# Regrouping k and q of the next batch earlier, and loading v in a step of its own, in a fused attention and mixer kernel

## The chip, the cores and the metric

The kernel runs on one core of one Trainium2 chip. The metric is device time in microseconds (us), from the start to the end of one execution; lower is better. The kernel is written with a manual schedule: each engine executes its instructions in the order in which the program issues them, and engines wait for each other through semaphores that the framework places where tiles are written and read. The engines are TensorE (PE in the profile), VectorE (DVE), ScalarE (ACT), GpSimd (POOL) and SyncE (SP). SP and POOL issue the DMAs.

## The reference

For 8 batches, 12 heads, 448 tokens and a head width of 64, a sigmoid attention without normalisation is followed by an MLP mixer over tokens and channels (d_model 768, token width 256, channel width 1536):

```
scores = (q @ k.T) / sqrt(64) - log(448)
x      = sigmoid(scores) @ v                    # heads side by side: 448 x 768 a batch
u      = x + (relu(x.T @ w_tok1) @ w_tok2).T
out    = u + relu(u @ w_ch1) @ w_ch2
```

Inputs and output are float32; the kernel loads and multiplies in float16 and accumulates in float32.

## The kernel before, in words

A batch is cut into three **units** (u = 0, 1, 2) of four heads. A **cycle** c = 3b + u works at unit u of batch b. The opening (cycles 0 to 5) and three cycles of transition (6 to 8, lines 1082 to 1138) lead to the main loop (cycles 9 to 23, batches 3 to 7, lines 1147 to 1206), whose order of work on PE is the table STEPS (lines 1141 to 1145), one row a unit. Its letters:

- **k**: one block of scores (qk, line 187): four matmuls of tr_k against tr_q into a PSUM tile, and a sigmoid on ACT (line 199) into one buffer of the ring att, 10 deep.
- **a4, a7**: attention times v (av, line 209) for the unit of the cycle before. DVE then casts the sum into xT (line 228), and after a7 SP issues a DMA transpose of xT into xn (xtrans_dma, line 241). In unit 2, a7 also has token_sums, four differences of u on DVE (line 446).
- **t, T**: the first token matmul (tok_tail, line 276, and tok1, line 295), reading the xn that was transposed one cycle earlier. At the end of each cycle ytrans (line 311) does the second token matmul, and DVE adds it to xT in the tile ut (line 325).
- **7** (unit 2 only): utrans (line 330), a DMA transpose of the whole ut into un (the rows of u that are added to the output), and sevens (line 1071), the 15 steps of the first channel matmul for the batch before, by seven products of sums (line 503). sums are combinations of c1, hsums of c2, made once from the weights (weight_sums, output_sums; lines 407 and 619); the list early holds these 24 pieces of DVE work, of which c2's are the last 12.
- **q6, r, L, 4, 5, 6**: second channel matmul of the batch before that (lines 373, 692, 712, 753). DVE adds un to the result (lines 576, 732, 778) and SP stores the output rows (line 589).
- **c**: takes up to two pieces from the list copies.

The list **copies** prepares k and q of the next batch. At the end of unit 0 it is filled by through_dma(b + 1, 0) (line 152) with eight pieces: three regroupings of k by DVE (relayout, line 134: raw_k to rel_k, one a unit), one DMA transpose of rel_k into tr_k (line 147, issued by SP), and then the same four for q. Before the change, unit 1 takes two at its first c (k0, k1) and two at the c that ends it (k2 and k's transpose); unit 2 takes two at its c (q0, q1), and sevens takes the last two after its steps 1 and 3 (q2, and q's transpose). So on SP's queue q's transpose stands behind un's.

Loads are issued by POOL (load, line 118), two DMAs a tensor and batch, with the cast from float32 to float16 on the way. gated_loads(b) (line 988), at the end of unit 2, first has POOL copy two elements of tr_q of batch b + 1 (line 990); that copy can only run when q's transpose has landed, and it holds back everything behind it on POOL's queue: v of batch b + 1, then k and q of batch b + 2. raw_k and raw_q have one buffer each, raw_v two.

Of the kernel before, what the change touches and what calls it, by code (L numbers as in the profile page):

```python
# [9 lines left out]
FP16 = mybir.dt.float16  # L10
# [11 lines left out]
NJ = 7  # L22
NP = 64
NU = 3
# [6 lines left out]
def kernel(  # L31
# [11 lines left out]
    nc = tc.nc  # L43

    B, H, S, E = q.shape
# [15 lines left out]
    pa = ctx.enter_context(tc.tile_pool(name="pa", bufs=2))  # L61
# [7 lines left out]
    c2 = pc.tile([128, NCB, D], FP16, name="c2")  # L69
    gate = pc.tile([128, 2], FP16, name="gate")  # L70
# [31 lines left out]
    raw, rel, tr = {}, {}, {}  # L102
    att, xn, h1, un = {}, {}, {}, {}
# [14 lines left out]
    def load(b, t, src, u0, u1):  # L118

        for g in range(2):  # L120
            dst = raw_tile(b, t)[64 * g : 64 * g + 64, u0:u1, :, :, :]
            heads = src[b, 6 * g + 2 * u0 : 6 * g + 2 * u1]
            nc.gpsimd.dma_start(
                out=dst.rearrange("p u hi j e -> p (u hi) (j e)"),
                in_=heads.rearrange("h (p j) e -> p h (j e)", j=NJ),
            )
# [58 lines left out]


    def qk(b, u, j):
        att[b, u, j] = pa.tile([128, 2, S], FP16, tag="att", bufs=10, name=f"att_{b}_{u}_{j}")
        ps = pp.tile([128, 2, 512], FP32, tag="qk", bufs=2, name=f"qk_{b}_{u}_{j}")
        for g in range(2):  # L190
            for hi in range(2):
                nc.tensor.matmul(  # L192
                    out=ps[64 * g : 64 * g + 64, hi, 0:S],
                    lhsT=tr[b, "k"][64 * hi : 64 * hi + 64, u, j, 64 * g : 64 * g + 64],
                    rhs=tr[b, "q"][64 * hi : 64 * hi + 64, u, :, 64 * g : 64 * g + 64],
                    start=True,
                    stop=True,
                )
        nc.scalar.activation(  # L199
            out=att[b, u, j][:, :, :],  # L200
            in_=ps[:, :, 0:S],
            func=SIGMOID,
            bias=bias_t[:, :],
            scale=att_scale,
        )
# [105 lines left out]
    def ytrans(b, u, banks=()):  # L311
        for g in range(2):
            db = NU * g + u
            if banks:
                at_bank[0] = banks[g]
            ps = bank([128, 512], FP32, f"yt_{b}_{db}")
            for tcb in range(2):
                nc.tensor.matmul(  # L318
                    out=ps[:, 0:S],
                    lhsT=h1[b, u][:, tcb, g, :],  # L320
                    rhs=w2[:, tcb, :, :],
                    start=(tcb == 0),
                    stop=(tcb == 1),
                )
            nc.vector.tensor_tensor(  # L325
                out=ut_of(b)[:, db, 0:S], in0=xT(b, u)[:, g, 0:S], in1=ps[:, 0:S], op=ADD
            )
# [462 lines left out]
    for g, queue in enumerate((nc.scalar, nc.sync)):  # L790
        queue.dma_start(
            out=first_q[64 * g : 64 * g + 64].rearrange("p hi j e -> p hi (j e)"),
            in_=q[0, 6 * g : 6 * g + 2].rearrange("h (p j) e -> p h (j e)", j=NJ),
# [28 lines left out]
    for par in range(2):  # L822
        part = slice(64 * par, 64 * par + 64)
        nc.gpsimd.dma_start(
            out=w1[part, 0:3, :],
            in_=tok_rows[0:6].rearrange("(t par) p c -> par p t c", par=2)[par],
# [4 lines left out]
        out=w2s[:, :, :], in_=moe_w_tok2.rearrange("(tc t) s -> t tc s", tc=2)  # L831
# [156 lines left out]
    def gated_loads(b):  # L988

        nc.gpsimd.tensor_copy(  # L990
            out=gate[:, :], in_=tr[b + 1, "q"][:, NU - 1, NJ - 1, 126:128]
        )
        if b > 1:
            load(b + 1, "v", v, 0, NU)
        for t, src in (("k", k), ("q", q)):
            if b + 2 < B:
                load(b + 2, t, src, 0, NU)

    ON_DMA = range(N_FIRST, N_CYCLES)

# [4 lines left out]
    early = weight_sums() + output_sums()  # L1005
    for c, cb in ((N_FIRST, 3), (N_FIRST + 1, 8)):
        b, u = divmod(c, NU)
# [63 lines left out]
    def sevens(b, banks=(2, 3, 0, 1, 0)):  # L1071
        step = ch1_seven(b, banks)
        for at, (n, gs) in enumerate(SEVENS):
            step(n, gs)
            if copies and at in (1, 3):
                copies.pop(0)()
            if early and at in (3, 5, 9):
                early.pop(0)()

    pending, copies = [], []  # L1080
# [1 line left out]
    for c in range(2 * NU, ONE_RUN):  # L1082
        b, u = divmod(c, NU)
        before, ahead = divmod(c - 1, NU), divmod(c - 2, NU)


        if c == 2 * NU:
            first = c
            pending, shares = [*pieces_ch2(0, by_half[2:]), *pieces_last(0)], [10, 10, 10]
            total = sum(w for w, f in pending)  # L1090
            spent = 0

        def work(share):
            goal = 3 * sum(shares[: c - first]) + share * shares[c - first]
            done = 0
            while pending and spent + done < total * goal / 90:
                w, f = pending.pop(0)
                if len(pending) % 4 == 3:
                    lane[0] ^= 1
                at_bank[0] = 2 + lane[0]  # L1100
                f()
                done += w
                if len(early) > 3 and (c > 2 * NU or len(early) > 12):
                    early.pop(0)()
                if copies:
                    copies.pop(0)()
            return done

        qk(b, u, 0)
        qk(b, u, 1)  # L1110
        at_bank[0] = 0
        av(*before)
        xtrans_dma(*before)
        qk(b, u, 2)
        if c == 2 * NU + 2:
            copies += through_dma(3, 0)[NU + 1 :]
        spent += work(1)
        qk(b, u, 3)
        qk(b, u, 4)
        at_bank[0] = 0  # L1120
        tok_tail(*ahead)
        tok1(*ahead, with_scores=True)
        if c == 2 * NU + 1:
            copies = through_dma(3, 0)[: NU + 1]
        spent += work(2)
        if c == 2 * NU + 2:
            utrans(b - 1)
            token_sums(b - 1)
        qk(b, u, 5)
        qk(b, u, 6)  # L1130
        spent += work(3)
        if u == 2:
            sevens(b - 1)
        at_bank[0] = 0
        ytrans(*ahead)
        if u == 2:
            gated_loads(b)
    assert not copies and not pending and not early

    X, Y = 2, 0  # L1140
    STEPS = (
# [3 lines left out]
    )  # L1145
    scores = ((b, u, j) for b in range(NU, B) for u in range(NU) for j in range(NJ))
    for c in range(ONE_RUN, N_CYCLES):
        b, u = divmod(c, NU)
        before, ahead = divmod(c - 1, NU), divmod(c - 2, NU)
        lot = b - 2  # L1150
        if u == 0:
            seven = ch2_seven(lot, X, X + 1, X + 1)
            seven.sums(0, 2)
        at_bank[0] = X
        if u == 2:
            steps, outputs = ch2_pair(lot, u)
        else:
            steps = seven.pair(((1, 2), (7, 3))[u])
        done = 0
        for x in STEPS[u].split():  # L1160
            if x == "k":
                qk(*next(scores))
            elif x[0] == "q":
                for n in range(int(x[1:])):
                    steps.pop(0)()
            elif x[0] == "a":
                at_bank[0] = Y
                av(*before, done, int(x[1:]))
                done = int(x[1:])
                if done == NJ:  # L1170
                    xtrans_dma(*before)
                    if u == 2:
                        token_sums(b - 1)
            elif x == "r":
                if u == 2:
                    outputs()
                else:
                    for n in ((1, 2), (3, 7))[u]:
                        seven.end(n)
                if u == 0:  # L1180
                    seven.sums(2, 4)
            elif x == "t":
                at_bank[0] = Y
                tok_tail(*ahead)
            elif x == "T":
                tok1(*ahead, with_scores=True)
            elif x == "L":
                at_bank[0] = X + 1
                for w, f in pieces_last(lot):
                    f()  # L1190
            elif x == "c":
                for n in range(2 if copies else 0):
                    copies.pop(0)()
            elif x == "7":
                utrans(b - 1)
                sevens(b - 1)
            else:
                seven.plain(int(x))
        assert not steps
        if u == 0 and b + 1 < B:  # L1200
            copies = through_dma(b + 1, 0)
        at_bank[0] = Y
        ytrans(*ahead)
        if u == 2 and b + 1 < B:
            gated_loads(b)
    assert not copies and not early and next(scores, None) is None
# [84 lines left out]
```

## Time and profile before

| | |
|---|---|
| median of 3 runs | 366.76 us (365.31 to 368.28) |
| the profiled execution | 369.44 us, of which 367.3 us are its span from first to last instruction |
| mean granted TensorE clock | 0.981 |
| busy | PE 345.1 us (94%), DVE 228.7 (62%), ACT 212.6 (58%), POOL 57.0 (16%) |
| PE waits for a DMA of xn | 11.0 us in 3 places, the longest 4.1 |
| PE waits for DVE's add into ut | 1.4 us in 3 places, the longest 1.0 |
| POOL waits at the gate of line 990 | 186.0 us in 6 places |
| issue to landing of the transposes, median | xn 3.9 us, tr_k 6.7, tr_q 5.9, un 6.7 |

PE is nearly always busy, so the first thing to look for is where it is not, and the next is who it waits for there. A busy PE also says nothing of its clock: the line of granted clock has to be read beside it. The waits of POOL are long because it has nothing else to do; they matter only through what stands behind them in its queue.

### The profile page before, as it was taken

How to read it: one execution, taken by the hardware profiler on the slowest of the kernel's cores; microseconds unless marked ns; L12 is line 12 of the kernel's file. 1: busy time of each engine (PE TensorE's matmuls, PEld its weight loads, DVE VectorE, ACT ScalarE, POOL GpSimd, SP SyncE). 2: the span in 40 equal slices, each digit the busy share in tenths (PEclk: the TensorE clock that was granted, in tenths of full speed). 3: DMA queues.
4: the chain of work that ended last, by engine and by line, in shares of the span. 5: the costliest groups of instructions: out<-in, count | busy, mean ns of one | idle time of the engine just before them, and what ended most of it. 6: DMA issues, size and time to landing. Idle time of an engine off the chain costs nothing.

```text
span 367.3 us, 10275 instructions
## 1 busy us (share of the span) xinstructions
PE 345.1 (94%) x4435; PEld 245.9 (67%) x4435; DVE 228.7 (62%) x462; ACT 212.6 (58%) x271; POOL 57.0 (16%) x98
## 2 busy tenths in 40 slices
PE   7998999998999999959999699977999999999985
PEld 4654565555976698636986379744797679756943
DVE  2465578778686657817587274862658454957661
ACT  4995842877477675727757185760948677111400
POOL 8893340310310004000040000400001000000000
PEclk9999999999999999969999899998999999999999
DMA  7999999999994888968989489895996248043414
GB/s 123 175 152 192 205 205 197 162 221 225 177 208 70 194 163 111 198 92 135 166 134 194 78 155 193 101 189 76 160 192 106 48 106 157 2 112 77 80 43 107
DMA packets 104380, 52.17 MB, mean 142 GB/s; under 512 B 76432, under 2 KB 101264, under 8 KB 104336
## 3 DMA queue, kind: packets, MB, share of 16 engines
q1 hardware_dynamic: 78944, 29.70, 45.6%
q0 software_dynamic: 25168, 21.50, 38.3%
q8 instruction: 34, 0.56, 0.6%
q10 hardware_dynamic: 224, 0.33, 0.3%
q14 instruction: 10, 0.08, 0.1%
HBM read 43.45 MB, written 11.01 MB: 148 GB/s over the span
## 4 chain that ended last, share of the span: by engine, by line
PE 65%; DMA 10%; DVE 2%; issue 0%
PE c_ab L503 13%; DMA xn<-xT 10%; PE c_c L503 8%; PE qk L192 6%; PE c L753 6%; PE c L692 6%; PE c L373 5%; PE xa L219 5%; PE c L712 4%; PE tk L295 4%; PE yt L318 3%; PE c L553 2%; PE c_a L503 1%; PE c_b L503 1%; PE tk L276 1%; DVE hid L678 0%
## 5 line engine op out<-in xcount | busy, mean ns | idle before, releaser
L199 ACT ACTIVATE att<-qk,att_bias 128x896 f16<-128x896 f32 x168 | 156.6, 1012 | 58.4 <-PE qk L192 57.8
L192 PE MATMUL qk<-tr_q,tr_k 64*64 64x448 f16 x672 | 60.0, 359 | 0.6 <-ACT att L199 0.2
L503 PEld LDWEIGHTS <-c 128*128 128x128 f16 x504 | 48.2, 98 | 1.5 <-issue 1.3
L228 DVE CAST xT<-xa 128x448 f16<-128x448 f32 x48 | 27.7, 619 | 32.4 <-PE xa L219 32.4
L219 PE MATMUL xa<-att,raw_v 64*64 64x448 f16 x672 | 41.4, 349 | 1.4 <-DVE ut L325 1.4
L192 PEld LDWEIGHTS <-tr_k 64*64 64x64 f16 x672 | 24.3, 105 | 23.8 <-issue 17.0
L503 PEld LDWEIGHTS <-sum 128*128 128x128 f16 x378 | 36.3, 98 | 0.0
L325 DVE TENSOR_TENSOR ut<-xT,yt 128x448 f16<-128x448 f16 x48 | 27.5, 613 | 5.1 <-PE yt L318 5.1
L990 POOL COPY gate<-tr_q 128x2 f16<-128x2 f16 x6 | 1.4, 234 | 186.0 <-DMA tr_q<-rel_q 186.0
L219 PEld LDWEIGHTS <-raw_v 64*64 64x64 f16 x672 | 23.7, 107 | 9.4 <-issue 2.9
L309 ACT ACTIVATE h<-tk 128x256 f16<-128x256 f32 x42 | 14.2, 393 | 26.9 <-PE tk L295 26.9
L524 ACT ACTIVATE pt_ab<-c_ab 128x896 f32<-128x896 f32 x21 | 19.3, 917 | 13.5 <-PE c_ab L503 13.5
L778 DVE TENSOR_TENSOR o<-un,c 64x384 f32<-64x384 f16 x12 | 6.6, 552 | 28.2 <-PE c L753 28.0
L373 PE MATMUL c<-c,h 64*64 64x384 f16 x480 | 23.3, 322 | 0.0
L295 PE MATMUL tk<-xn,w 128*128 128x256 f16 (+1 forms) x156 | 22.9, 284 | 0.1
L318 PE MATMUL yt<-w,h 128*128 128x448 f16 x96 | 22.2, 353 | 0.3 <-DVE ut L325 0.3
L553 PE MATMUL c<-c,h 128*128 128x384 f16 x120 | 22.0, 326 | 0.0
L753 PE MATMUL c<-c,h 128*64 128x384 f16 x192 | 21.8, 387 | 0.0
L533 DVE TENSOR_TENSOR h<-pt_ab,c_ab 128x896 f16<-128x896 f32 x14 | 15.2, 1084 | 9.5 <-PE c_ab L503 9.5
L526 ACT ACTIVATE h<-c_ab 128x896 f16<-128x896 f32 x7 | 6.4, 917 | 24.4 <-PE c_ab L503 24.4
L533 DVE TENSOR_TENSOR h<-pt_c,c_c 128x448 f16<-128x448 f32 x21 | 13.0, 617 | 10.6 <-PE c_c L503 10.6
L373 PEld LDWEIGHTS <-h 64*64 64x64 f16 x480 | 16.4, 107 | 3.7
(102 smaller groups left out, 538.0 us busy)
## 6 DMA issues: line engine op xcount, KB each, us to landing
out_dram<-o SPq DMA_DIRECT2D x48, 192.0 KB, 2.8
c<-in_moe_w_ch_dram POOLq DMA_DIRECT2D x4, 1152.0 KB, 16.2
raw_k<-in_k_dram POOLq DMA_DIRECT2D x10, 336.0 KB, 7.9
raw_q<-in_q_dram POOLq DMA_DIRECT2D x10, 336.0 KB, 10.8
raw_v<-in_v_dram POOLq DMA_DIRECT2D x10, 336.0 KB, 5.7
out_dram<-o SPq DMA_DIRECT2D x15, 96.0 KB, 2.2
raw_q<-in_q_dram POOLq DMA_DIRECT2D x12, 112.0 KB, 4.7
raw_k<-in_k_dram POOLq DMA_DIRECT2D x12, 112.0 KB, 4.7
```

What stands on the lines that cost most here:

```text
L192: nc.tensor.matmul(out=ps[64 * g : 64 * g + 64, hi, 0:S], lhsT=tr[b, "k"][64 * hi : 64 * hi + 64, u, j, 64 * g : 64 * g + 64], rhs=tr[b, " ...
L199: nc.scalar.activation(out=att[b, u, j][:, :, :], in_=ps[:, :, 0:S], func=SIGMOID, bias=bias_t[:, :], scale=att_scale,)
L219: nc.tensor.matmul(out=ps[g][64 * hi : 64 * hi + 64, 0:S], lhsT=raw[b, "v"][64 * g : 64 * g + 64, u, hi, j, :], rhs=att[b, u, j][64 * g : ...
L228: nc.vector.tensor_copy(out=xT(b, u)[:, g, 0:S], in_=ps[g][:, 0:S])
L295: nc.tensor.matmul(out=ps[tcb], lhsT=w1[rows, t, cols], rhs=xn[b, u][rows, :, t, :], start=(t == 0 and not with_scores), stop=(t == (2 if ...
L318: nc.tensor.matmul(out=ps[:, 0:S], lhsT=h1[b, u][:, tcb, g, :], rhs=w2[:, tcb, :, :], start=(tcb == 0), stop=(tcb == 1),)
L325: nc.vector.tensor_tensor(out=ut_of(b)[:, db, 0:S], in0=xT(b, u)[:, g, 0:S], in1=ps[:, 0:S], op=ADD)
L373: nc.tensor.matmul(out=ps[p][m : m + 64, 0:n], lhsT=lhsT(p, part, m), rhs=rhs(p, part), start=(first and turn == 0), stop=(last and turn = ...
L503: nc.tensor.matmul(out=ps[:, g, p, :], lhsT=weights[n][:, d, 128 * cb : 128 * cb + 128], rhs=moving[n][:, d, :], start=(n in (1, 5, 2) and ...
L533: nc.vector.tensor_tensor(out=shaped(dst), in0=shaped(parts[gs, which]), in1=ps, op=ADD)
L553: nc.tensor.matmul(out=ps[:, 0:DH], lhsT=h2[b][:, BY_GROUP[cb], 128 * t : 128 * t + 128], rhs=c2[:, BY_GROUP[cb], cols], start=(cb == 0), ...
L753: nc.tensor.matmul(out=ps[g], lhsT=h2[b][:, BY_GROUP[n], 384:448], rhs=c2[:, BY_GROUP[n], DH * g : DH * g + DH], start=(n == 0), stop=(n = ...
```

## The change

In the main loop, the regroupings and the transpose of q move forward: unit 1 takes k0, k1 at its first c and k2, k's transpose and q0 at its last; unit 2 takes q1, q2 and q's transpose right behind its first block of scores. q's transpose thereby stands ahead of xn's, of a store and of un's on SP's queue. v of the next batch gets a gate of its own (gated_v): POOL copies two elements of rel_k of the next batch as unit 1 ends, and v's two loads follow it, ahead of the gate for k and q. Only for batch 3 does v still come behind the gate on tr_q. The DVE pieces of c2's sums are taken at other points: fewer in cycle 7, five instead of three in sevens, and the last three in cycles 9 and 10. The ring att has 11 buffers in place of 10. No matmul, activation or DMA of data is added or removed; POOL gets four more gate copies.

```diff
-        att[b, u, j] = pa.tile([128, 2, S], FP16, tag="att", bufs=10, name=f"att_{b}_{u}_{j}")
+        att[b, u, j] = pa.tile([128, 2, S], FP16, tag="att", bufs=11, name=f"att_{b}_{u}_{j}")
...
-        if b > 1:
+        if b == 2:
             load(b + 1, "v", v, 0, NU)
         for t, src in (("k", k), ("q", q)):
             if b + 2 < B:
                 load(b + 2, t, src, 0, NU)
+
+    def gated_v(b):
+
+        nc.gpsimd.tensor_copy(out=gate[:, :], in_=rel[b, "k"][:, NU - 1, NJ - 1, 0, 0:2])
+        load(b, "v", v, 0, NU)
...
-            if early and at in (3, 5, 9):
+            if early and at in (3, 5, 6, 9, 13):
                 early.pop(0)()
...
-                if len(early) > 3 and (c > 2 * NU or len(early) > 12):
-                    early.pop(0)()
                 if copies:
                     copies.pop(0)()
+                elif len(early) > (12 if c == 2 * NU else 8):
+                    early.pop(0)()
...
-        "k k q6 k c a4 k a7 k q6 r k t T L 4 c",
-        "k k q6 k c q6 k a4 k a7 k q6 k q6 r k t k T 7",
+        "k k q6 k c2 a4 k a7 k q6 r k t T L 4 c3",
+        "k c3 k q6 k q6 k a4 k a7 k q6 k q6 r k t k T 7",
...
         for x in STEPS[u].split():
+            if early and x in ("r", "T"):
+                early.pop(0)()
...
-            elif x == "c":
-                for n in range(2 if copies else 0):
+            elif x[0] == "c":
+                for n in range(int(x[1:]) if copies else 0):
                     copies.pop(0)()
...
         ytrans(*ahead)
+        if u == 1 and b + 1 < B:
+            gated_v(b + 1)
         if u == 2 and b + 1 < B:
             gated_loads(b)
```

More of the change, by code (lines that the diff above doesn't have):

```diff
@@ L1137 @@
             gated_loads(b)
-    assert not copies and not pending and not early
+    assert not copies and not pending
     X, Y = 2, 0
```

## The prediction

> **What bounds the kernel now.** I read, in this order: the page's busy shares, PE's waits, the chain of waits in order of time, the windows around one wait, and the timelines of POOL and SP there. PE is busy 94% of the span and the chain runs over it nearly everywhere, so what counts is where PE is not busy, or busy slowly.
>
> ```profile
> PE 345.1 (94%) x4435; PEld 245.9 (67%) x4435; DVE 228.7 (62%) x462; ACT 212.6 (58%) x271; POOL 57.0 (16%) x98
> PEclk9999999999999999969999899998999999999999
> ```
>
> PE's own waits have two places of weight: three waits for the transposed xn, and in all 1.4 us for DVE's add into ut (one of 1.05 us, at 83 us).
>
> ```profile
> PE tk L276 <- DMA xn<-xT: 11.0, 3, 4.1
> PE xa L219 <- DVE ut L325: 1.4, 3, 1.0
> ```
>
> The chain in order of time (start, length, what) shows one undisturbed batch of the main loop and one with the wait. L712 at 104.67, 143.80 and 189.28 is the same step of batches 3, 4 and 5; tk and L753 are the same matmuls in unit 1 of each batch.
>
> ```profile
> 104.67 0.97 PE c L712 x24
> ...
> 117.39 0.76 PE tk L295 x6
> 118.15 2.07 PE c L753 x24
> ...
> 143.80 0.97 PE c L712 x24
> ...
> 148.10 12.02 DMA xn<-xT
> 160.60 1.40 PE tk L295 x6
> 161.99 3.71 PE c L753 x24
> ...
> 189.28 0.97 PE c L712 x24
> ```
>
> Batch 3 takes 143.80 - 104.67 = 39.13 us. The chain has the same step at 233.49 and 278.53, so batches 4, 5 and 6 take 45.48, 44.21 and 45.04. Batch 7, from there to its last yt at 316.40, takes 37.87, exactly as batch 3 to its yt at 142.54. So 39.13 is what a batch costs when nothing is late, seen twice, and the excess is 6.35 + 5.08 + 5.91 = **17.3 us**. PE's timeline gives its parts: waits of 3.76, 3.20 and 4.09 us (11.05), and a slow stretch behind each: the 24 matmuls of L753 take 3.71, 3.75 and 3.21 in place of 2.07. The windows show why (columns: PE, PEld, DVE, ACT, POOL, granted clock, DMA share, GB/s): DMA is full up to the wait, and the clock is at half behind it.
>
> ```profile
> 147.00:150.00 3.00, 3.00 (x46) 2.21 (x38) 2.93 (x8) 2.71 (x5) 0.00 (x0) 1.00 1.27 205
> 156.00:159.00 3.00, 0.41 (x12) 0.01 (x3) 1.28 (x4) 1.53 (x2) 0.00 (x0) 0.91 1.36 113
> 159.00:162.00 3.00, 1.83 (x12) 0.95 (x14) 0.00 (x0) 0.38 (x1) 0.00 (x0) 0.50 0.57 125
> ```
>
> What fills the DMA engines is in POOL's timeline: the gate opens at 142.33 and six loads of 336 KB are issued, 5 us ahead of xn's transpose at 148.10. Of the 20 transposes of xn the shortest landed in 3.0 us, the median in 3.9; this one needed 12, and PE wants it at 156.4.
>
> ```profile
> 142.33 0.18 POOL L990 COPY gate<-tr_q 128x2 f16<-128x2 f16 x1 [40.19 <-DMA tr_q<-rel_q]
> 142.78 1.36 POOL L123 DMA_DIRECT2D raw_v<-in_v_dram  x2 [0.27 <-PE c_c L503]
> 144.12 1.35 POOL L123 DMA_DIRECT2D raw_k<-in_k_dram  x2
> ```
>
> The gate waits for q's transpose, the last of four on SP in unit 2:
>
> ```profile
> 123.33 3.76 SPq L147 DMA_TRANSPOSE tr_k<-rel_k  x1
> 128.09 1.61 SPq L242 DMA_TRANSPOSE xn<-xT  x1
> ...
> 132.06 4.20 SPq L332 DMA_TRANSPOSE un<-ut  x1
> 136.37 3.89 SPq L147 DMA_TRANSPOSE tr_q<-rel_q  x1
> ```
>
> Batches 3 and 7 have no such wait. For batch 7 the gate (277.69) releases v alone. For batch 3 all six loads were issued, but from 97.45 on, 11.5 us ahead of the transpose at 108.97: in cycle 8 q's transpose (89.82) already stands ahead of un's (93.80) on SP. That is the order that the change gives the other batches.
>
> **The change part by part.** Times are those of batch 3 before.
>
> *v behind k's regrouping.* rel_k is complete at 122.5 (DVE's timeline: the third copy starts at 121.90, 0.61 us). v's loads then go out at about 123 instead of 142.8, 20 us earlier. The six loads from 142.78 hold xn back until 160.17, that is 17.4 us less its own 3.9: 13.5 us for six, 4.5 for v's two. The longest wait is 4.09. So v's move alone takes the three waits away, by a margin of 0.4 us at the worst. POOL's part (four gate copies of 0.18 us) costs nothing: POOL waits 186.0 us at its gates.
>
> *q's transpose ahead.* q2 is regrouped at about 125 instead of 133.43; SP is free of k's transpose at 127.1, so q's is issued from 127.1 to about 130.6. Landing: median 5.9, so 133; with v's 4.5 us ahead of it, 137.5. Then the gate opens, 5 to 9 us earlier than 142.33, and k's and q's loads (four, 9.0 us) are through at 142 to 147. xn's transpose at 148.10 finds the DMA engines free. The three waits and their slow stretches go: **-17.3 us**. What is late next there: nothing up to 39.13 a batch, as batches 3 and 7 show.
>
> What moves behind it on SP, each up to 3.5 us: xn of unit 1 from 128.09 to about 130.6, wanted by PE at 147.87: hidden. The store of o_2, wanted by nobody until its buffer is reused three tiles on: hidden. un's transpose from 132.06 to about 133 to 136, landing in 6.7 (longest of seven 7.8), so at 140 to 144, and DVE wants un at 147.95 (L732): hidden by 4 us; without that cover 1 us late is 1 us a batch in three batches (rival A).
>
> *DVE.* q0's copy (0.53 us from start to start) now stands ahead of the two adds into ut, which end at 124.1 instead of 123.57; the PSUM banks that they free are wanted by av's matmuls at 124.89. Hidden by 0.8 us; with no cover, 0.5 us in each of four batches, 2 us. q1 and q2 follow until 125.2, and the next cast wants DVE at 126.64. sevens loses q2's copy, which is a gain of at most 0.5 us on DVE and none on PE, as PE never waits there. In batches 4 to 6, DVE also had to wait for raw_k (rel_k at 243.90, 1.66 us); with k loaded earlier that goes, off the path.
>
> *c2's sums.* In cycle 7 DVE has seven pieces of hsum between 76.8 and 82.9 ahead of the adds into ut, and PE waits 1.05 us at 83.52 for them. The instruction order of the changed kernel has three there: 4 x 0.47 = 1.9 us less, so the wait of 1.05 goes: **-1.0 us**. Two pieces are added in sevens of cycle 8, one just before the adds at 104.50, and three in cycles 9 and 10: av's second half wants its bank 0.25 us before DVE would have freed it, and the product of L692 at 109.64 waits for an add that ended at 109.4 and now ends at 109.9. **+0.4 us**, between 0 (idle of DVE takes them in) and 5 x 0.47 = 2.4.
>
> *att 11 deep.* In every row of STEPS the av that frees the tenth buffer stands ahead of the score that needs it, on PE's own queue, and PE waits 0.2 us for ACT in the whole run: 0, between -0.2 and 0.
>
> **Sum:** -17.3 - 1.0 + 0.4 = -17.9 us; the profiled execution goes from 369.44 to 351.5, its span from 367.3 to 349.4. The median is 2.68 below the profiled execution. If that is fixed, the median comes to 348.9; if it was the size of the waits, which now go, to 351.5. I take **350**, between.
>
> The Trainium skill, on the page "TensorE: Matmul & The Clock Gate" (Part 1), says that one idle window of about 3.4 us halves the clock and about 3.4 us of work restores it. An estimate by it is half of 3.4, 1.7 us, a wait, 5.1 for three, where the rows show 17.3 - 11.05 = 6.3; the sum would be 16.7 in place of 17.9. The trace agrees on the half (0.50) and roughly on the threshold: a wait of 3.20 us cost it too.
>
> **The rivals.**
>
> *A: un comes late.* k's and q's loads now run beside un's transpose. If they share the engines evenly, un, issued until about 137, lands after the loads' 9.0 us and about 4 of its own: 150, which is 2.2 us late in each of the three batches that load k and q; PE's L692 follows on that add: 350 + 6.6 = **357**. The wait of 1.05 us at 83 lost no clock and the one of 3.20 did; 2.2 lies between, and I count none (with it, 2.1 more each: 363). Against it: un of cycle 8 was issued from 93.80 to 98.07 with all six loads from 97.45, and landed within 7.8 us, the longest of all; what is issued ahead of the loads was not held up, what came behind them was. For it: DMA has about 26 us of full work for the 25 us from 123 to 148 (the windows of 120 to 144 sum to 3.8 MB, six loads are 2.06, and full is 205 GB/s).
> The Trainium skill says on the page "DMA: Bandwidth & Descriptors" (Queues, rings and completion order) that each DMA engine takes packets in turn from the queues that have work. By that rule alone this rival would be the likelier; xn's 12 us behind loads agrees better with first come, first served.
>
> *B: q's transpose comes late, and the kernel is slower.* v's loads are now ahead of k's and q's transposes, which the next batch's first score needs at 143.23. Expected at 137.5, so the slack is 5.7 us. It decides the sign when the four batches lose more than the 17.9 gained: 4.5 us each, of which about 2.1 would be slow clock (6.3 / 3), so a wait of 2.4 and a landing at 145.6, 18.5 us after the issue. The longest landing of any transpose, behind all six loads, is 12.3. If it happens, say 5 us of wait and 2.1 of clock in each: 350 + 28 = **378**.
>
> *C: it does not do what it says.* The gates open earlier, but the loads still run into xn's transpose, since the DMA is the bound. If the whole backlog is merely moved, the three waits stay and only c2's sums gain: **366**. Against it: one batch moves 6.5 MB (windows 144 to 189), 31.5 us at 205 GB/s, of 39.13.
>
> **How the numbers follow.** Forecast 0.76, A 0.13, B 0.07, C 0.04. The forecast's own range is 347 to 353: 348.9 and 351.5, with 2 on either side for the DVE terms. A range that holds 8 in 10 takes in A: 346.5 to 358. A measurement of this kernel tells about 1% (3.7 us) from no change; forecast and A are faster (0.89), C is the same (0.04), B is slower (0.07).
>
> **What would show it.** Right: no wait of tk for xn, granted clock 1.00 throughout the main loop, every batch 39.1 us between its L712 steps, POOL's gates opening near 122 and 135 (on batch 3's clock), the wait at 83 us gone. Wrong: a wait of DVE's L732 for un, of qk L192 for tr_q, or of xa L219 for ut in unit 2; or a batch over 40 us with its DMA share at 1.27 throughout.

## The result, and the profile after

The changed kernel takes 399.95 us (median of 4 runs, 398.78 to 401.36) against 367.4 for the kernel before on the same chip: a ratio of 1.090, with a 95% interval of 1.083 to 1.096. The forecast was 350, between 346.5 and 358. It is 9% slower, not 5% faster. Times here and below are medians of the fast executions of a kernel; the few slow ones, up to 543 us in one control, are left out.

The page of the profile after (span, and the granted clock) shows four dips of the clock where there were three:

```profile
span 398.8 us, 10273 instructions
PEclk9999999999999996999859999679998899999999
```

Who waited for whom, after (total us, times, longest):

```profile
DVE ut L325 <- DMA un<-ut: 43.6, 4, 15.0
PE xa L219 <- DVE ut L325: 39.6, 7, 13.8
```

The waits of tk for xn, 11.0 us before, are not in the list any more: that part came as forecast. In their place DVE waits for un's transpose, in all four batches that are followed by another, and it waits with the add into **ut**, not with the add of un into the output. ut is one buffer. un's transpose reads it, and the add of the next batch's first unit (ytrans at the end of unit 2) overwrites it. DVE executes in order, so everything behind that add stops too, and PE soon stands at av, whose PSUM banks (the memory that matmuls write to) the add would have freed. The DVE timeline after, at the end of batch 3:

```profile
149.60 1.15 DVE L325 TENSOR_TENSOR ut<-xT,yt 128x448 f16<-128x448 f16 x2 [6.84 <-DMA un<-ut]
```

The chain after, in order of time (L712 is the same step of unit 1 in batches 3 to 7):

```profile
112.13 0.97 PE c L712 x24
139.38 10.13 DMA un<-ut
...
160.40 0.97 PE c L712 x24
...
187.97 17.56 DMA un<-ut
...
215.73 0.97 PE c L712 x24
...
243.57 16.75 DMA un<-ut
```

The batches take 48.27 and 55.33 here, and by the further marks at 270.43 and 318.36 then 54.70 and 47.93, against 39.13 undisturbed: an excess of 9.1 + 16.2 + 15.6 + 8.8 = 49.7 us. The sum closes: 367.3 - 17.3 (the xn waits, gone) + 49.7 = 399.7, and the span is 398.8. Of the 49.7, 39.6 are PE's waits at av, and about 10 are work at half clock behind them: in the windows (columns as before) the clock falls to 0.50.

```profile
147.00:150.00 3.00, 0.00 (x0) 0.00 (x0) 0.40 (x1) 0.00 (x0) 0.00 (x0) 0.83 1.28 203
150.00:153.00 3.00, 2.72 (x27) 1.48 (x29) 1.78 (x4) 0.08 (x1) 0.00 (x0) 0.50 1.01 162
```

Why un comes late is in the timelines of SP and POOL after (start, length on the queue):

```profile
123.01 9.83 SPq L147 DMA_TRANSPOSE tr_k<-rel_k  x1
132.95 3.26 SPq L147 DMA_TRANSPOSE tr_q<-rel_q  x1
...
139.38 4.33 SPq L332 DMA_TRANSPOSE un<-ut  x1
```

```profile
122.36 1.32 POOL L123 DMA_DIRECT2D raw_v<-in_v_dram  x2 [0.27 <-issue]
...
140.69 1.31 POOL L123 DMA_DIRECT2D raw_k<-in_k_dram  x2 [0.35 <-issue]
```

k's transpose, issued beside v's two loads, holds SP for 9.83 us where it took 3.76 before. So un is issued at 139.4 instead of 132.1 (about 1 us of this is q's transpose, now ahead of it: with k's transpose at its old length un is issued at 133.06, in a run below). Then k's and q's loads come beside it: 1.3 us behind un's issue in batch 3, where un lands after 10.13 us, and 0.3 us ahead and 0.6 us behind in batches 4 and 5, where it needs 17.56 and 16.75.

### The profile page after: what moved, and what is told of

Its sections match the earlier page's. It is cut to its first block, busy times and chain, and to the rows that moved or that the text cites. A ratio compares the mean times of both kernels' runs of the same rounds, so it can differ in the third digit from the quotient of the medians.

```text
span 398.8 us, 10273 instructions
## 1 busy us (share of the span) xinstructions
PE 350.4 (88%) x4435; PEld 248.2 (62%) x4435; DVE 230.0 (58%) x462; ACT 213.6 (54%) x271; POOL 57.3 (14%) x102
## 4 chain that ended last, share of the span: by engine, by line
PE 72%; DMA 14%; DVE 6%; ACT 3%; issue 2%; SPq 1%; DVEq 0%; ACTq 0%
DMA un<-ut 13%; PE xa L219 10%; PE c_ab L503 10%; PE qk L192 8%; PE c L692 7%; PE c L373 6%; PE c_c L503 5%; PE tk L295 5%; PE c L553 5%; PE c L753 4%; PE c L712 4%; PE yt L318 3%; ACT att L199 3%; PE c L350 2%; DVE ut L325 2%
## 5 line engine op out<-in xcount | busy, mean ns | idle before, releaser
L199 ACT ACTIVATE att<-qk,att_bias 128x896 f16<-128x896 f32 x168 | 158.2, 1009 | 99.2 <-PE qk L192 98.6
L219 PE MATMUL xa<-att,raw_v 64*64 64x448 f16 x672 | 49.8, 387 | 39.6 <-DVE ut L325 39.6
L192 PE MATMUL qk<-tr_q,tr_k 64*64 64x448 f16 x672 | 65.9, 372 | 0.4 <-DVE tr_k L184 0.2
L219 PEld LDWEIGHTS <-raw_v 64*64 64x64 f16 x672 | 26.7, 115 | 52.7 <-issue 44.0
L325 DVE TENSOR_TENSOR ut<-xT,yt 128x448 f16<-128x448 f16 x48 | 27.5, 615 | 47.9 <-DMA un<-ut 43.6
L192 PEld LDWEIGHTS <-tr_k 64*64 64x64 f16 x672 | 26.3, 109 | 23.5 <-issue 15.9
L295 PE MATMUL tk<-xn,w 128*128 128x256 f16 (+1 forms) x156 | 21.8, 274 | 0.1
L732 DVE TENSOR_TENSOR o<-un,c 128x384 f32<-128x384 f16 x28 | 15.2, 552 | 5.8 <-PE c L692 3.6
L503 PE MATMUL c_ab<-diff,c 128*128 128x224 f16 x168 | 18.4, 259 | 0.0
L295 PEld LDWEIGHTS <-w 128*128 128x128 f16 (+1 forms) x156 | 13.4, 97 | 7.1 <-issue 4.4
```

The source lines that it names most:

```text
L192: nc.tensor.matmul(out=ps[64 * g : 64 * g + 64, hi, 0:S], lhsT=tr[b, "k"][64 * hi : 64 * hi + 64, u, j, 64 * g : 64 * g + 64], rhs=tr[b, " ...
L199: nc.scalar.activation(out=att[b, u, j][:, :, :], in_=ps[:, :, 0:S], func=SIGMOID, bias=bias_t[:, :], scale=att_scale,)
L219: nc.tensor.matmul(out=ps[g][64 * hi : 64 * hi + 64, 0:S], lhsT=raw[b, "v"][64 * g : 64 * g + 64, u, hi, j, :], rhs=att[b, u, j][64 * g : ...
L295: nc.tensor.matmul(out=ps[tcb], lhsT=w1[rows, t, cols], rhs=xn[b, u][rows, :, t, :], start=(t == 0 and not with_scores), stop=(t == (2 if ...
L325: nc.vector.tensor_tensor(out=ut_of(b)[:, db, 0:S], in0=xT(b, u)[:, g, 0:S], in1=ps[:, 0:S], op=ADD)
L503: nc.tensor.matmul(out=ps[:, g, p, :], lhsT=weights[n][:, d, 128 * cb : 128 * cb + 128], rhs=moving[n][:, d, :], start=(n in (1, 5, 2) and ...
```

## The experiments

Theory W: the loss is the overwriting of ut, which waits for un's transpose; un is late for two reasons, v's loads beside k's transpose (which delay all that follows on SP) and k's and q's loads beside un's own. Rival D: the DMA engines have too much to do in these 25 us, whatever the order. Rival V: v's new place alone is at fault. Rival Q: it is the regroupings on DVE.

**Two buffers for ut.**

```diff
-        ... name=f"ut{n}") for n in range(2)
+        ... name=f"ut{n}") for n in range(3)
-        return uts[min(b, 1)]
+        return uts[0 if b == 0 else 1 + (b - 1) % 2]
```

> The changed kernel with two buffers for ut that batches take in turn, and the ring att cut to 8 buffers to pay for the memory. Theory W (the loss is DVE's add into ut for the next batch, which has to wait until un's transpose has read the one ut buffer): the 43.6 us of that wait go, and with them av's 39.6 us; un itself lands at about the same time, 7 to 9 us later than the add would have come, so DVE's L732, which comes 4.8 us after the add, still waits some 2 to 4 us in three batches: 350 to 365 us. Rival D (the DMA engines have too much work in these 25 us, whatever waits for them): the wait only moves on to L732 or to the next xn, and the time stays above 380.

Measured: 387.4 us, ratio 1.052 (1.044 to 1.061). The wait at ut is gone, but one of about half its size stands now at the first reader of un, as a line of its waits shows:

```profile
DVE o L732 <- DMA un<-ut: 22.5, 3, 10.6
```

Theory W's number missed: un lands 15.4 to 18.2 us after its issue in these three batches, so the 4.8 us that the second buffer buys are less than half of its lateness, and L732 waits up to 10.6 us, not 2 to 4. Rival D's number fits, and the later runs had to decide whether its reason does.

The control, the kernel before with the same two buffers and the same shorter ring:

> Control for the run with two buffers for ut: the kernel before with the same two buffers and the ring att at 8. The old waits for xn stay and nothing is gained by the second buffer: 366 to 371 us, the upper part if the shorter ring costs something.

Measured: 366.9 us, ratio 0.998 (0.994 to 1.002). So neither the buffer nor the ring at 8 costs or gives anything on the kernel before. On the changed kernel the ring of 8 is not quite free: there ACT waits 7.1 us for av to give back a buffer, and PE's scores 3.9 us for ACT, so up to 4 of the 387.4 us may be the ring's.

**v's loads back behind the gate on tr_q,** the rest as changed.

```diff
-        if b == 2:
+        if b > 1:
             load(b + 1, "v", v, 0, NU)
...
-        if u == 1 and b + 1 < B:
-            gated_v(b + 1)
```

> The changed kernel with v's loads back behind the gate on tr_q. Theory W with its first half (v's loads make the issue of k's transpose on SP slow, 9.8 us in place of 3.8, and so delay q's, xn's and un's): k's transpose takes 3.8 us of SP again, un is issued at about 133 on batch 3's clock instead of 139.4, but now six loads go out at about the same moment and un is held by them for longer: waits at ut of about 10 us in batches 3 to 5, 380 to 395 us. If only v's place did the harm (rival V), the time comes to 350 to 358.

Measured: 397.5 us, ratio 1.079 (1.074 to 1.084): a little above the range. k's transpose is back at 3.82 us, un is issued at 133.06, and now all six loads are issued from 133.05 on. The chain has what un needed to land then, in batches 3, 4 and 5, and in batch 6, where v's two loads are the only ones and go out 1.2 us ahead of it:

```profile
133.06 23.57 DMA un<-ut
188.59 20.25 DMA un<-ut
240.00 23.39 DMA un<-ut
296.11 10.20 DMA un<-ut
```

V falls: with v back the loss is nearly whole. What v no longer does to k's transpose, it does to un.

**un's transpose ahead of q's again,** the rest as changed (q's transpose right behind utrans):

```diff
-        "k c3 k q6 k q6 ...
+        "k c2 k q6 k q6 ...
                 utrans(b - 1)
+                while copies:
+                    copies.pop(0)()
                 sevens(b - 1)
```

> The changed kernel with un's transpose ahead of q's again; v, the regroupings and c2's sums as changed. Theory W: un is still issued some 3 us later than before, since v's loads slow k's transpose, but has no k and q loads beside it, which wait for q's transpose: un is read by 142 to 144, so the wait at ut is 0 to 2 us a batch. q's transpose then lands at about 145 to 147, where the next score wants it at 143, 2 to 4 us of wait in four batches: 355 to 370 us. Rival Q (the regroupings of q on DVE, not the transposes, are what hurts): stays near 400.

**Only v's loads moved,** on the kernel before:

> The kernel before with v's loads alone moved to the end of unit 1, as in the change. The forecast on record was that this alone removes the waits for xn (350). Theory W: it does, but k's transpose takes 8 to 10 us of SP, and un and q's transposes come 6 us later than before: wait at ut 0 to 2 us a batch, and q's transpose lands 2 to 4 us after the next score wants it: 355 to 370 us.

Measured: 372.4 (ratio 1.010, 1.006 to 1.015) and 371.2 (1.009, 1.006 to 1.013), both a little above their ranges, which end at 370. The waits at ut fall to 2.1 and 1.0 us in all, and those for xn are gone. Instead PE waits for q's transpose; the first line is of the run with un first, the second of the run with v alone:

```profile
PE qk L192 <- DMA tr_q<-rel_q: 15.6, 4, 4.1
```

```profile
PE qk L192 <- DMA tr_q<-rel_q: 13.8, 4, 3.9
```

The two differ in the regroupings of q on DVE and in c2's sums, and not in time: Q falls. v's loads at the end of unit 1 give the kernel nothing, since what they take from xn's waits they put on k's transpose, and so on q's.

**k's and q's loads let go by un's transpose,** the rest as changed:

```diff
-        nc.gpsimd.tensor_copy(
-            out=gate[:, :], in_=tr[b + 1, "q"][:, NU - 1, NJ - 1, 126:128]
-        )
+        if b > 2:
+            held_by = un[b - 1][:, NDB - 1, 3, 126:128]
+        else:
+            held_by = tr[b + 1, "q"][:, NU - 1, NJ - 1, 126:128]
+        nc.gpsimd.tensor_copy(out=gate[:, :], in_=held_by)
```

> The changed kernel with k's and q's loads let go when un's transpose has landed, in place of q's transpose. It takes the loads off un's transpose and leaves v's loads on k's. Theory W: k's transpose still takes 8 to 10 us of SP and un is issued at about 139, but lands in 6 to 8 us: wait at ut 3 to 4 us in four batches, some with slow clock: 362 to 378 us. If k's and q's loads did no harm (rival V), it stays near 400.

Measured: 375.8 us, ratio 1.022 (1.016 to 1.029). un lands in 6.7 to 8.0 us, and av's wait for ut goes from 39.6 to 17.4 us: this is what v's loads cost through SP alone. Its row of DVE's wait:

```profile
DVE ut L325 <- DMA un<-ut: 20.8, 4, 7.3
```

**v's loads at the start of unit 1,** the rest as changed. The gate copies from the first regrouping of k:

```diff
-        ... in_=rel[b, "k"][:, NU - 1, NJ - 1, 0, 0:2])
+        ... in_=rel[b, "k"][:, 0, NJ - 1, 0, 0:2])
```

with gated_v(b + 1) behind k0 in unit 1 in place of the end of unit 1.

> The changed kernel with v's loads moved to the start of unit 1, so that only k's and q's loads, let go by q's transpose, meet another transpose. Theory W: k's transpose takes 3.8 us of SP, un is issued at about 133, four loads go out at the same moment, and un is held by them: it lands 15 to 18 us after its issue, at 148 to 151, where DVE's add into ut wants it read at 143: wait of 5 to 8 us in three batches with slow clock, none in the fourth, which has no such loads: 370 to 382 us. Rival V (v's place alone was at fault): 349 to 353.

Measured: 382.1 us, ratio 1.041 (1.035 to 1.048). k's transpose takes 3.87 us again, and un, with four loads beside it, needs 19.39, 14.12 and 18.66 us; the loads go out less than 0.1 us from un's issue in the first and third case and 1.8 us ahead of it in the second. This is the other half alone. The wait of DVE at ut, and un in the chain:

```profile
DVE ut L325 <- DMA un<-ut: 26.7, 3, 10.7
```

```profile
133.77 19.39 DMA un<-ut
185.23 14.12 DMA un<-ut
230.94 18.66 DMA un<-ut
```

The wait is 26.7 us here and 20.8 in the run before it: together 47.5, against 43.6 with both.

**Both mended:** v's loads at the start of unit 1, and k's and q's loads behind un.

> The changed kernel with v's loads at the start of unit 1 and with k's and q's loads let go by un's transpose in place of q's. All transposes are then free of loads: no wait at ut, xn, un or tr_q of more than 1 us: 348 to 353 us, as with v's loads alone moved. If anything else in the change costs time (DVE's order, SP's order), it comes out above 353.

Measured: 351.3 us, ratio 0.957 (0.952 to 0.963). The same transposes and loads, with q's regrouping and transpose as early as in the change, run without a wait of PE of more than 0.3 us in the main loop, and its L712 steps of batches 4 to 7 come 39.13 to 39.14 us apart, as in an undisturbed batch. So rival D falls: the work fits, its order did not. The four runs with q early make a square: 351.3 us with neither disturbance, 375.8 and 382.1 with one, 400.0 with both. The two excesses, 24.5 and 30.8 us, sum to 55.3, where both together cost 48.7. The timeline of SP in that run shows all four transposes at their undisturbed length:

```profile
124.78 3.97 SPq L147 DMA_TRANSPOSE tr_k<-rel_k  x1
128.85 3.78 SPq L147 DMA_TRANSPOSE tr_q<-rel_q  x1
132.74 1.25 SPq L242 DMA_TRANSPOSE xn<-xT  x1
...
135.32 4.46 SPq L332 DMA_TRANSPOSE un<-ut  x1
```

**v's loads at the start of unit 1 on the kernel before,** with the transposes in their old places, and then the same with c2's sums and att as changed:

> The kernel before with v's loads moved to the start of unit 1, behind the first regrouping of k, where the DMA engines carry 0 to 0.7 of their share; the transposes keep their order and their places. Theory W: v's loads (9 us of POOL and DMA from about 114) are through before k's transpose is issued at 123, which then takes 3.8 us of SP again; un and q's transposes keep their times, k's and q's loads go out at 142 as before, but only four of them, so xn lands 3 to 5 us earlier and the three waits go: 349 to 353 us. Rival D (the DMA engines are too full for any such move): a wait at xn, at tr_q or at ut of some us a batch stays, 358 to 370.

> The same with c2's sums spread and att 11 deep as in the change: 0 to 1 us less than with v's loads alone, 348 to 352.

Measured: 352.1 (ratio 0.961, 0.955 to 0.966) and 351.2 (0.958, 0.953 to 0.963). Moving v's two loads to where the DMA engines are nearly idle is the whole gain. Of the change, the early q adds nothing to it: 351.2 without it, 351.3 with it. The windows of the kernel before show the place (v's loads go out at 114.67 in the first of the two runs), and the row of that run's granted clock has no dip left:

```profile
111.00:114.00 3.00, 3.00 (x45) 1.65 (x47) 2.58 (x6) 1.12 (x2) 0.00 (x0) 1.00 0.71 100
114.00:117.00 3.00, 3.00 (x68) 2.31 (x70) 1.60 (x3) 3.00 (x4) 0.00 (x0) 1.00 0.00 0
117.00:120.00 3.00, 3.00 (x42) 1.92 (x33) 1.14 (x4) 1.94 (x4) 0.00 (x0) 1.00 0.55 104
```

```profile
PEclk9999999999999999999999999999999999999999
```

**c2's sums and att alone,** on the kernel before:

> The kernel before with c2's sums spread as in the change and att 11 deep, nothing else. The term on record was -1.0 + 0.4 us and 0 for att: 366 to 367.5, not to be told from the kernel before. In the trace the wait of 1.05 us of av for ut in cycle 7 is gone.

Measured: 367.0 us, ratio 1.001 (0.998 to 1.005). The trace has the forecast step:

```profile
PE xa L219 <- DVE ut L325: 0.3, 2, 0.2
```

This wait was 1.4 us before; in time it is lost in the interval.

**Only k's loads beside un,** v at the start of unit 1 and q behind un:

> The changed kernel with v's loads at the start of unit 1, k's loads let go by q's transpose (so beside un's) and q's loads only by un's. Two loads then meet un, where four (382 us) and none (351 us) were run. If a transpose is held by the loads beside it in proportion (six: 20 to 24 us to landing, four: 14 to 19, none: 6.7, so 2.8 us a load), un lands 12 us after its issue at 133, at 145: a wait at ut of 1 to 3 us in three batches, too short for the clock: 355 to 362 us. If any load at all holds the whole transpose until the loads' queue is empty, the wait is near that of four: 370 to 380.

Measured: 369.8 us, ratio 1.014 (1.005 to 1.023), between the two expectations. un in the chain of that run:

```profile
133.73 14.74 DMA un<-ut
180.66 10.36 DMA un<-ut
220.71 14.71 DMA un<-ut
```

The first and third had their loads issued 0.04 and 0.06 us behind un's transpose (133.77 and 220.77), the second 1.19 us behind (181.85): in this one case 1.2 us of lead is worth 4.4 us of landing. So the hold grows with the loads. Issued within 0.2 us of them, un lands after 14.7 us beside two, 18.7 and 19.4 beside four, 23.4 and 23.6 beside six, against 6.7 beside none, so two already cost nearly half of what six do. The lead counts as much as the number: the 10.13 us of batch 3 in the run of the change had four loads, but 1.3 us behind.

## Why the prediction was wrong, by its own steps

**The step that failed** is the term for un's transpose: "landing in 6.7 (longest of seven 7.8), so at 140 to 144, and DVE wants un at 147.95 (L732): hidden by 4 us". Both halves of it were wrong.

The deadline: the first to wait for that transpose is not who reads its result but who overwrites its source, the add into ut, 4.8 us earlier in the same DVE timeline that was read for the sum:

```profile
143.16 1.15 DVE L325 TENSOR_TENSOR ut<-xT,yt 128x448 f16<-128x448 f16 x2
...
147.95 0.56 DVE L732 TENSOR_TENSOR o<-un,c 128x384 f32<-128x384 f16 x1
```

With the 140 to 144 that the same sentence gave for un's landing, the cover was -1 to 3 us, not 4. Had the landing been right, this would have cost at most 1 us a batch.

The landing is the larger half: a second buffer for ut leaves 387.4 us, and with un landing early the one buffer does with 351.3. It was off for two reasons that the runs separate. "SP is free of k's transpose at 127.1" took the old 3.76 us for an instruction that now had loads beside it; it took 9.83, and this alone is worth 20.8 us of waits at ut (375.8 us). With it q's transpose was issued at 132.95, and the gate for k's and q's loads opened at 140.15, beside un's issue, where the sum had it open by 137.5. And un's own landing, put at 6.7 to 7.8, was 10.1 to 17.6 us with four loads beside it; this alone is worth 26.7 us of waits (382.1 us). The wait of xa L219 for ut, which the prediction named among its signs of being wrong, is the one that came.

**Rival A had the place and the mechanism** (un beside k's and q's loads) but was given 0.13, on the strength of a row that did not bear on the case: un of cycle 8 had a lead of 3.7 us on its loads (93.80 against 97.45), so nearly all of its 4.3 us on SP was over when they began. In the main loop un comes later behind q's transpose, by xn, a store and the sums it waits for, and the lead is -0.3 to 1.3 us. The rival's price, 2.2 us a batch, also used the wrong deadline. Its 26 us of DMA work fit the windows of 123 to 144; the 3.8 MB that it names, from 120 on, would be 28.6 us with the six loads.

The Trainium skill says on the page "DMA: Bandwidth & Descriptors" (Queues, rings and completion order) that each DMA engine takes packets in turn from the queues with work. This spoke for that rival, and the runs agree in kind: a transpose issued first was held by two or four loads issued 0.04 to 0.6 us behind it. "First come, first served" does not hold for them.

**Rival B had the other half**: v's loads ahead of k's transpose. But it looked for the wait at the next batch's score, and the run has none there. k's transpose landed up to 15.3 us after its issue, where the prediction argued from a longest landing of 12.3; the wait came at ut, through SP's queue. The wait that B meant is the one of the two runs in which q's transpose stands behind un's with v's loads early (15.6 and 13.8 us).

**v's term** ("v's move alone takes the three waits away") was right about xn and wrong about the sum: the 4.5 us that v's loads put on xn they put on k's transpose instead, with 4 to 7 us on SP. Where they meet no transpose, the term is confirmed: 352.1 us, and a span of 350.2 against 367.3 us with no wait for xn.

**Right as forecast:** the excess of 17.3 us and its removal (351.2 to 352.1 us where nothing new waits, against the forecast 350); the clock at half behind a long wait (0.50 behind the one of batch 3); the wait at 83 us gone with c2's sums, although too small to be timed; DVE's regroupings, POOL's gates and att free of cost.

**What stays open:** how the loads hold a transpose. Its time on SP's queue grows with them (4.3 us to 13 or 14 for un), so part of the delay is already in its issue, but the runs do not separate that from the sharing of the engines. What a lead is worth rests on single batches.

## What to carry to other kernels

When a DMA is moved, look up two deadlines: who reads what it writes, and who next overwrites what it reads. With a single buffer the second can be the earlier, and it stops an engine that executes in order.

A transfer that is moved out of one collision has to be followed to the next one: ask which DMA is issued within its length at the new place, and choose a stretch in which the DMA rows of the windows are low, as the start of unit 1 was here.

A row that is to show that two transfers do not disturb each other must have them as close in time as they will be; a lead of 3.7 us showed nothing about a lead of 0.

## What the runs showed of the hardware

A DMA transpose that is issued beside loads holds up its own queue. un's 24 blocks took 4.3 us of SP alone; with loads of 336 KB issued within 0.2 us of it, 8.8 and 11.3 beside two, 13.1 and 13.6 beside four, 13.9 and 14.5 beside six. It landed after 6.7, 14.7, 18.7 to 19.4 and 23.4 to 23.6 us. Everything behind it on SP waits until its time there is over. Four loads delayed un by 12.0 and 12.7 us, no less than they need themselves: in the run with both mended the DMA engines are busy with the same four and one transpose of xn for about 10 us (145 to 155).
